# Turning two thirds of an inverse spectrum by copies through DRAM instead of by VectorE, with a new planned order

## The chip, the core and the metric

The kernel runs on one core of a Trainium2 chip. The core has a matrix engine (TensorE, PE in the profile), a vector engine (VectorE, DVE), an activation engine (ScalarE, ACT), a general engine (GpSimd, POOL) and a synchronising engine (SyncE, SP) that here only issues transfers; sixteen DMA engines move data between DRAM and the on-chip memory SBUF. Matmul results land in PSUM. The metric is the time of one execution on the device in microseconds (us), lower being better. The kernel before took 353.0 us in the median of three runs (352.21 to 354.79).

## The reference

Two branches work on the same input `u` (2048 positions, 640 channels) and are mixed by a gate. Branch A is a state-space layer: a kernel `K` of 2048 taps is built for each channel from complex parameters, and `u` is convolved with it by a Fourier transform of length 4096. Branch B is a gated MLP with a spatial matrix `w_sp` of 2048 x 2048.

```python
g = _sigmoid((x * gate_w).sum(-1, keepdims=True))
# A: convolution of u with K by FFT of length 2 L, plus a skip
P = jnp.exp(logdA[:, :, None] * l[None, None, :])
K = jnp.einsum('dn,dnl,dn->dl', Cc, P, dB).real
Yf = rfft2(pad(u)) * rfft2(pad(K))
y = irfft2(Yf)[:, :, 0, :L] + u * Dskip
# B
z = _gelu(jnp.einsum('bsd,df->bsf', x, w_in))
g2 = jnp.einsum('ts,bsf->btf', w_sp, layernorm(z[..., Fh:])) + b_sp
b = jnp.einsum('bsf,fd->bsd', z[..., :Fh] * g2, w_out)
return g * a + (1 - g) * b
```

## The kernel before

**A planner sets the order.** Every piece of work is recorded with `add` (or `dma`, `evac`, `actf`, which call it): the engine or engines that may do it, a cost, what it reads and writes, and a bias. `Plan.run` then goes through a modelled time, picks on each engine the ready task with the highest value of remaining chain plus bias, and emits the instructions in that order. Dependences in the plan are by named keys, such as `("vs", 0, k)`. The emitted program gets its semaphore waits from the tiles' memory, not from these keys. The table `TUNE` at the head of the file adds a number to the bias of single lines (function, line within it, and a loop index or `None`); it was found by a search.

**The convolution.** The 640 channels are split in two groups, `h = 0` with 480 channels and `h = 1` with 160. The transform of length 4096 is done in stages with matmuls:

- `s1_u` (u) and `conv_s1` (K) do the first stage and store its results to the DRAM tensors `FU_d` and `FK_d`. The stage's result is copied out of PSUM by `evac` into `s1u` or `s1k`.
- `conv_s2(h)` runs over 32 values of `k`, singly for `h = 0`, two at a time for `h = 1`. Each step loads its part of the spectra (`fu`, `fk`), does the second stage (`ps_u`, `ps_s2k`, line 1188), multiplies the two spectra on VectorE (`p12`, line 1190), does the first inverse stage with the table `G` (`ps_v`, line 1196), and ScalarE copies it into `X["vs"][h][:, k, :]` (line 1198). So `vs` holds 128 rows by 32 values of `k` by the channels of the group.
- `conv_vt(g)` turns `vs`: within each block of 32 partitions the partition index and `k` change places. VectorE does this in place by 32x32 transposes, two bf16 channels taken as one 32-bit word, 40 channels of one block at a time (line 1204). `g` = 0, 1, 2 are the three lots of 160 channels of `h = 0`, four transposes each; `g` = 3 is `h = 1`.
- `conv_i2(h)` does the last inverse stage with the table `HT` (lines 1278 and 1280), eight groups of output rows for `h = 0` and four for `h = 1`. `i2_out` scales by the gate and adds to branch B's part: VectorE directly from PSUM for one half (line 1212), ScalarE into `tm` and VectorE or GpSimd for the other (lines 1229 and 1231).

**Around it.** Branch B's spatial product (`sp_block`, `ps_g` line 812, `ps_o` line 832) fills PE for most of the time up to 264 us. Its last rows stay in the tile `acc`, the earlier ones go to DRAM (`ob_d`) and are read back before the last stage.

**Transfers.** `dma` issues on SP, or, where `QQ` stands, on SP or POOL as the planner likes. [...]

The order at the end of `main` in which work is recorded:

```python
    conv_s2(0)
    add("NONE", 0.0, open_cv1, w=["cv1"] + par, deps=cva_ids + kf1_ids + t_ids)
    xk, wk = k_expand(1)
    conv_s1(1, xk, wk)
    for g in range(3):
        conv_vt(g)
    conv_s2(1)
    conv_vt(3)
    oo = ob_load()
    conv_i2(0, oo)
    conv_i2(1, oo)
```

Of the kernel before, what the change touches and what calls it, by code (L numbers as in the profile page):

```python
# [25 lines left out]
class Handle:  # L26
# [9 lines left out]


TUNE = {
    ('conv_s1', 15, ('g', 0)): -1398,
    ('conv_s1', 15, None): 3878,  # L40
    ('conv_s2', 35, ('h', 0)): 10715,
    ('conv_s2', 34, ('h', 0)): 12557,
    ('conv_s2', 34, ('h', 1)): 10661,
    ('conv_s2', 28, None): -730,
    ('conv_s2', 42, None): 11507,
    ('eights', 6, None): 22869,
    ('eights', 13, None): 9278,
    ('i2_out', 15, None): 2641,
    ('k_expand', 28, ('h', 1)): -13135,
    ('k_exps', 10, ('c', 4)): -5933,  # L50
    ('k_exps', 10, None): -2461,
    ('k_store', 13, ('h', 1)): -2592,
    ('k_store', 14, None): -14209,
    ('k_store', 6, None): 2313,
    ('k_tables', 31, ('c', 4)): 1745,
    ('k_tables', 31, None): 2593,
    ('k_tables', 32, ('c', 3)): -6618,
    ('k_tables', 32, None): -5389,
    ('k_tables', 41, ('c', 3)): -7569,
    ('k_tables', 29, ('c', 3)): 19395,  # L60
    ('k_tables', 29, ('c', 7)): 107,
    ('k_tables', 29, None): -29059,
    ('k_tables', 6, ('c', 2)): -1107,
    ('k_tables', 6, None): -36,
    ('k_tables', 18, ('c', 5)): 11204,
    ('k_tables', 18, None): 3646,
    ('k_tables', 17, ('c', 3)): -6816,
    ('k_tables', 17, None): 2377,
    ('k_tables', 36, ('c', 0)): 6700,
    ('k_tables', 36, ('c', 7)): -59230,  # L70
    ('k_tables', 36, None): -4043,
    ('k_tables', 38, None): -15448,
    ('main', 151, ('g', 0)): 41152,
    ('main', 151, ('g', 1)): 3118,
    ('main', 151, ('g', 2)): 1052,
    ('main', 149, None): 37766,
    ('main', 148, None): 1429,
    ('main', 147, None): 3632,
    ('main', 156, None): 2671,
    ('main', 159, None): -8713,  # L80
    ('main', 370, None): -17765,
    ('main', 369, None): -1820,
    ('main', 442, None): 125,
    ('main', 445, None): 3317,
    ('main', 413, None): -4292,
    ('quads', 10, None): 798,
    ('s1_u', 13, ('n0', 12)): -14799,
    ('s1_u', 13, ('n0', 2)): -11216,
    ('s1_u', 16, ('n0', 12)): -1100,
    ('s1_u', 16, ('n0', 2)): -2702,  # L90
    ('s1_u', 16, ('n0', 4)): -8304,
    ('s1_u', 16, None): -26814,
    ('s1_u', 20, ('h', 1)): 37644,
    ('s1_u', 3, ('n0', 0)): -28168,
    ('s1_u', 3, None): 2258,
    ('s1_u', 18, ('h', 1)): -33016,
    ('s1_u', 14, None): -24028,
    ('sp_block', 23, ('tb', 4)): -6232,
    ('sp_block', 23, None): 6779,
    ('sp_block', 25, None): 2910,  # L100
    ('sp_block', 20, ('tb', 0)): 13918,
    ('sp_block', 20, None): -32605,
    ('sp_block', 42, ('tb', 4)): -3738,
    ('sp_block', 42, ('tb', 5)): -4450,
    ('sp_block', 47, ('tb', 3)): 6173,
    ('sp_block', 3, ('tb', 1)): -8813,
    ('sp_block', 3, ('tb', 2)): 26644,
    ('sp_block', 3, ('tb', 7)): -26408,
    ('sp_block', 8, None): -13664,
    ('sp_block', 6, None): -1104,  # L110
    ('sp_block', 5, ('tb', 7)): -23479,
    ('sp_block', 5, None): -15147,
    ('tg_build', 15, None): 6085,
    ('tg_build', 20, None): 11595,
    ('x_group', 3, ('g', 0)): -1523,
    ('x_group', 3, ('g', 1)): -4918,
    ('x_group', 3, None): -1876,
    ('z1_tile', 10, ('g', 0)): 17523,
    ('z2_tile', 18, ('h', 1)): -43258,
    ('z2_tile', 10, None): -1119,  # L120
}
HELPERS = ("dma", "actf", "evac", "<lambda>", "ptt", "pts", "ftt", "fts", "pstt", "S_", "E", "K_", "M_")

# [1 line left out]
class Plan:  # L125
# [195 lines left out]
def kernel(  # L321
# [833 lines left out]
    def conv_s2(h):  # L1155
# [6 lines left out]
        for k in range(0, 32, NK):  # L1162
# [86 lines left out]
    def conv_i2(h, oo):  # L1249
        W, dsl = GW[h], slice(GO[h], GO[h] + GW[h])  # L1250
        nn = (1, 2)[h]
        for u, n in enumerate(range(0, NS, 2 * nn)):
# [28 lines left out]
            if u == 0:  # L1281
# [95 lines left out]
```

## Time and profile before

| | busy us | share of the span |
|---|---|---|
| span of the profiled execution | 352.3 | |
| PE matmul | 312.7 | 89% |
| VectorE (DVE) | 285.1 | 81% |
| ScalarE (ACT) | 245.2 | 70% |
| GpSimd (POOL) | 86.3 | 25% |
| transfers: q1 (SP) / q0 (POOL), of 16 DMA engines | 54.89 MB / 4.48 MB | 63.9% / 6.2% |

The busy shares are means over stages that differ much. The page's chain, followed back from the end, spends 49% of the span on PE, 20% on VectorE, 13% on ScalarE and 6% on SP's issues; its largest VectorE lines are the products `p` (line 1190) and the transposes `vs` (line 1204), 5% each. [...]

### The profile page before, as it was taken

The page shows a single profiled execution, that of the slowest core. Times are in us where ns is not written, and L with a number is a line of the kernel's source. Part 1 is how long each engine was busy: PE and PEld are TensorE (multiplying, and loading weights), DVE is VectorE, ACT ScalarE, POOL GpSimd, SP SyncE. Part 2 cuts the span into 40 slices and gives each one's busy share as a digit, 9 for nine tenths or more (in the row PEclk, how much of TensorE's full clock was granted, in tenths as well). Part 3 has the DMA queues.
Part 4 walks back from the last instruction along what each step waited for, and adds up shares of the span by engine and source line. Part 5 has one row for each costly group of instructions (what it writes and reads, how often), then busy time and mean ns, then how long its engine had stood idle before and what let it go on. Part 6 is the DMA issues. An engine that isn't in the chain of part 4 may idle for free.

```text
span 352.3 us, 8350 instructions
## 1 busy us (share of the span) xinstructions
PE 312.7 (89%) x3231; PEld 218.7 (62%) x3237; DVE 285.1 (81%) x560; ACT 245.2 (70%) x440; POOL 86.3 (25%) x107
## 2 busy tenths in 40 slices
PE   3899899989999999999999999699999999709982
PEld 3455455767766877878866988476774334406751
DVE  4079996799899599993799699327669999996985
ACT  1877648999996489999986671327558879604842
POOL 3007242000000041000440063427459200303220
PEclk9999999999999999999899999699999999976998
DMA  7979878788575596686296249989869866372404
GB/s 197 209 135 233 173 195 210 206 144 212 168 186 143 112 181 190 162 198 207 78 117 173 82 61 135 163 231 251 241 186 288 245 199 177 97 220 95 141 28 130
DMA packets 108580, 59.89 MB, mean 170 GB/s; under 512 B 75914, under 2 KB 105002, under 8 KB 108542
## 3 DMA queue, kind: packets, MB, share of 16 engines
q1 hardware_dynamic: 106030, 54.89, 63.9%
q0 software_dynamic: 2512, 4.48, 6.2%
q8 instruction: 25, 0.41, 0.5%
q14 instruction: 13, 0.11, 0.1%
HBM read 25.25 MB, written 19.47 MB: 127 GB/s over the span
## 4 chain that ended last, share of the span: by engine, by line
PE 49%; DVE 20%; ACT 13%; SPq 6%; issue 4%; DMA 4%; ACTq 0%; DVEq 0%
PE ps_g L812 21%; PE ps_o L832 6%; SPq L408 6%; PE ps_z L624 6%; ACT mr L415 5%; DVE p L1190 5%; DVE vs L1204 5%; PE ps_k L1046 3%; PE ps_k L1045 3%; PE ps_s2k L1188 3%; PE ps_v L1196 2%; DVE bst L604 2%; PE ps_s1k L1134 2%; ACT ET L415 1%; ACT L415 1%
## 5 line engine op out<-in xcount | busy, mean ns | idle before, releaser
L812 PE MATMUL ps_g<-wT,z2n 128*128 128x256 bf16 (+1 forms) x896 | 109.2, 278 | 1.7 <-DVE vT L816 1.2
L812 PEld LDWEIGHTS <-z2n 128*128 128x128 bf16 (+1 forms) x896 | 90.8, 104 | 18.7 <-issue 3.9
L1190 DVE TENSOR_TENSOR p<-ps_s2k,us 128x960 bf16<-128x960 f32 (+1 forms) x48 | 48.3, 1042 | 2.0 <-PE ps_s2k L1188 1.0
L993 POOL COPY ET<-mr 128x80 bf16<-128x80 bf16 x7 | 9.8, 1407 | 133.0 <-PE ps_k L1046 126.9
L832 PE MATMUL ps_o<-Wout,vT 128*128 128x320 bf16 (+1 forms) x224 | 33.8, 299 | 0.9 <-DVE vT L818 0.5
L624 PE MATMUL ps_z<-xg,Win 128*128 128x512 bf16 (+1 forms) x134 | 31.2, 379 | 1.4 <-ACT gl L598 1.1
L415 ACT ACTIVATE ET<-ci 128x640 bf16<-128x640 int16 (+1 forms) x40 | 25.7, 678 | 9.5 <-DVE ci L361 9.5
L592 PE MATMUL ps_z<-Win,xT 128*128 128x432 bf16 (+1 forms) x160 | 31.1, 353 | 1.0 <-ACT gl L598 1.0
L1046 PE MATMUL ps_k<-ET 128*32 128x33 bf16 x640 | 28.4, 258 | 3.9 <-issue 3.8
L1046 PEld LDWEIGHTS <-ET 128*32 128x32 bf16 x640 | 27.7, 195 | 3.3 <-issue 3.2
L1045 PEld LDWEIGHTS <-ET 128*32 128x32 bf16 x640 | 27.3, 192 | 2.6 <-issue 1.9
L1045 PE MATMUL ps_k<-ET 128*32 128x33 bf16 x640 | 28.8, 259 | 0.0
L832 PEld LDWEIGHTS <-vT 128*128 128x128 bf16 (+1 forms) x224 | 21.7, 97 | 10.2 <-issue 1.0
L1198 ACT CAST vs<-ps_v 128x480 bf16<-128x480 f32 (+1 forms) x48 | 24.4, 524 | 5.0 <-PE ps_v L1196 4.1
L1196 PE MATMUL ps_v<-p,G 128*128 128x480 bf16 (+1 forms) x128 | 25.2, 303 | 1.6 <-DVE p L1190 0.8
L816 DVE TENSOR_TENSOR vT<-ps_g,br 128x512 bf16<-128x512 f32 (+1 forms) x32 | 19.1, 617 | 8.6 <-PE ps_g L812 8.6
L1188 PE MATMUL ps_s2k<-fk,T 128*128 128x480 bf16 (+1 forms) x128 | 25.1, 306 | 0.2
L592 PEld LDWEIGHTS <-xT 128*128 128x128 bf16 x160 | 15.8, 99 | 15.3 <-issue 2.3
L415 ACT ACTIVATE mr<-lre 128x320 bf16<-128x320 f32 x66 | 25.0, 458 | 0.3 <-DVE ET L1017 0.2
L422 ACT CAST us<-ps_u 128x480 bf16<-128x480 f32 (+1 forms) x48 | 24.1, 523 | 0.8 <-ACT vs L1198 0.6
L624 PEld LDWEIGHTS <-Win 128*128 128x128 bf16 (+1 forms) x140 | 14.2, 101 | 16.1 <-issue 1.4
L422 ACT CAST s1k<-ps_s1k 128x960 bf16<-128x960 f32 (+1 forms) x15 | 13.0, 890 | 16.0 <-PE ps_s1k L1134 5.7
(192 smaller groups left out, 585.1 us busy)
## 6 DMA issues: line engine op xcount, KB each, us to landing
FU_d<-s1u SPq DMA_DIRECT2D x16, 240.0 KB, 3.0
fu<-FU_d SPq DMA_DIRECT2D x16, 240.0 KB, 2.9
fk<-FK_d SPq DMA_DIRECT2D x16, 240.0 KB, 3.0
z_d<-zt SPq DMA_DIRECT2D x24, 128.0 KB, 2.0
z1t<-z_d SPq DMA_DIRECT2D x8, 384.0 KB, 4.6
xf<-in_A_u_dram SPq DMA_DIRECT2D x8, 320.0 KB, 3.4
FK_d<-s1k SPq DMA_DIRECT2D x5, 480.0 KB, 5.4
Win<-in_B_w_in_dram SPq DMA_DIRECT2D x2, 1080.0 KB, 6.0
```

What stands on the lines that cost most here:

```text
L415: return add("ACT", cost, lambda e: act.activation(out=out_(), in_=in_(), func=func, scale=scale), r=r, w=w, fset=fs, bias=bias, deps=deps ...
L422: (vec.tensor_copy if e == "DVE" else act.copy)(out=out_(), in_=in_())
L592: pe.matmul(ps()[:, h, 0:432 + h], lhsT=xT[:, i, 128 * st:128 * st + 128], rhs=Win2[:, i, 432 * h:432 * h + 432 + h], start=(i == 0), stop ...
L624: pe.matmul(ps()[0:fs, ft - f0, :], lhsT=Win1[:, i, 128 * ft:128 * ft + fs], rhs=xg()[:, i, :], start=(i == 0), stop=(i == ND - 1))
L812: pe.matmul(ps()[0:fs, ft - f0, :], lhsT=z2n[:, st, 128 * ft:128 * ft + fs], rhs=wT()[:, st, :], start=(st == 0), stop=(st == NS - 1))
L832: pe.matmul(ps()[:], lhsT=vT[ft // 2]()[0:fs, ft % 2, 128 * r:128 * r + 128], rhs=Wout[0:fs, ft, HD * h:HD * h + HD], start=(ft == 0), sto ...
L1045: pe.matmul(o_, lhsT=ET[:, 0:32, d], rhs=M2[:, :, d], start=True, stop=False, tile_position=(0, 32 * q))
L1046: pe.matmul(o_, lhsT=ET[:, NA:NA + 32, d], rhs=E2[:, :, d], start=False, stop=True, tile_position=(0, 32 * q))
L1188: pe.matmul(ps()[:, i, W * n:W * n + W], lhsT=TK(k + n, i), rhs=fk()[:, j + n, :], start=True, stop=True)
L1190: add("DVE", dv1(2 * NW), lambda e, p12=p12, ps=ps, us=us: vec.tensor_tensor(out=p12()[:, :, 0:NW], in0=ps()[:, :, 0:NW], in1=us()[:, 0:NW ...
L1196: pe.matmul(pv()[:, W * n:W * n + W], lhsT=GV(k + n, i), rhs=p12()[:, i, W * n:W * n + W], start=(i == 0), stop=(i == 1))
L1198: add("ACT", 0.15 + NW / 1170, lambda e, k=k, pv=pv: act.copy(out=X["vs"][h][:, k:k + NK, :], in_=pv()[:, 0:NW].rearrange("p (k d) -> p k ...
```

## The change

Of the 480 channels of `h = 0`, the first 320 (`VD`) are no longer turned by VectorE. Each time four values of `k` have been copied into `vs`, a transfer stores these channels to a new DRAM tensor `VK_d`, whose first index is `k`, whose second is the partition and whose third is the channel. When all eight stores are done, sixteen transfers load them back into the same places of `vs`, now with `k` on the partition and the old partition (within its block of 32) as the second index: for each of four blocks `q`, for each half `w`, and for two groups `m` of eight rows. The last inverse stage of the first eight rows needs the loads of `m = 0` only. The remaining 160 channels are still turned by four VectorE transposes. The purpose is to take eight of twelve transposes off VectorE. At the same time the whole `TUNE` table is replaced by another one, found by a search; every line of it differs.

```diff
 TUNE = {
-    ('conv_s1', 15, ('g', 0)): -1398,
-    ('conv_s1', 15, None): 3878,
-    ('conv_s2', 35, ('h', 0)): 10715,
...
+    ('conv_i2', 37, ('h', 0)): 1844,
+    ('conv_i2', 39, ('h', 1)): -2564,
+    ('conv_i2', 39, None): -6223,
...
 }
...
     FK_d = [dram.tile([16, 4, 2, 32, w], BF, name=f"FK_d{w}") for w in GW]
+    VD = 320
+    VK_d = dram.tile([32, P, VD], BF, name="VK_d")
...
             add("ACT", 0.15 + NW / 1170, lambda e, k=k, pv=pv: act.copy(out=X["vs"][h][:, k:k + NK, :], in_=pv()[:, 0:NW].rearrange("p (k d) -> p k d", k=NK)), r=[pv, "cvb"], w=[("vs", h, k)], bias=S2E)
+            if h == 0 and k % 4 == 3:
+                dma(QQ, lambda k=k: VK_d[k - 3:k + 1, :, :].rearrange("k m d -> m k d"), lambda k=k: X["vs"][0][:, k - 3:k + 1, 0:VD], 1024 * VD, r=[("vs", 0, k - z) for z in range(4)], w=[("VK", k // 4)], bias=S2B, run=2 * VD)
+
+    def conv_vd():
+        NG = 2
+        g4 = 16 // NG
+        for m in range(NG):
+            for q in range(4):
+                for w in range(2):
+                    i0 = 16 * w + g4 * m
+                    dma(QQ, lambda q=q, i0=i0: X["vs"][0][32 * q:32 * q + 32, i0:i0 + g4, 0:VD], lambda q=q, i0=i0: VK_d[:, 32 * q + i0:32 * q + i0 + g4, :], 1024 * VD // NG,
+                        r=[("VK", i) for i in range(8)], w=[("vd", q, m, w)], bias=6500, run=640)
...
-            vk = [("va", 3, b) for b in range(4)] if h else [("va", g, b) for g in range(3) for b in range(4)]
+            vk = [("va", 3, b) for b in range(4)] if h else [("va", g, b) for g in range(VD // 160, 3) for b in range(4)] + [("vd", q, n // 8, w) for q in range(4) for w in range(2)]
...
-    for g in range(3):
+    conv_vd()
+    for g in range(VD // 160, 3):
         conv_vt(g)
```

More of the change, by code (lines that the diff above doesn't have):

```diff
@@ L38 @@
 TUNE = {
-    ('conv_s1', 15, ('g', 0)): -1398,
-    ('conv_s1', 15, None): 3878,
-    ('conv_s2', 35, ('h', 0)): 10715,
[L42 to L120, printed above, removed]
+    ('conv_i2', 37, ('h', 0)): 1844,
+    ('conv_i2', 39, ('h', 1)): -2564,
+    ('conv_i2', 39, None): -6223,
@@ new lines @@
+    ('conv_s2', 43, None): -17523,
+    ('conv_s2', 35, ('h', 0)): 633,
+    ('conv_s2', 35, ('h', 1)): 993,
+    ('conv_s2', 34, ('h', 0)): 24993,
+    ('conv_s2', 34, None): -4152,
+    ('conv_s2', 27, ('h', 0)): 2880,
+    ('conv_s2', 14, None): -40,
+    ('conv_s2', 28, None): -7269,
+    ('conv_s2', 42, None): -2974,
+    ('conv_vt', 4, None): -1249,
+    ('eights', 6, None): -4248,
+    ('i2_out', 7, None): -4434,
+    ('k_exps', 7, None): 83,
+    ('k_exps', 10, ('c', 0)): -406,
+    ('k_exps', 10, ('c', 4)): 573,
@@ new lines @@
+    ('k_store', 14, None): -2870,
+    ('k_store', 6, ('h', 1)): -12388,
+    ('k_store', 6, None): 8586,
+    ('k_sub', 23, None): -10732,
+    ('k_sub', 13, None): -11315,
+    ('k_tables', 31, ('c', 3)): 220,
+    ('k_tables', 31, ('c', 5)): 1445,
+    ('k_tables', 31, ('c', 7)): -6456,
+    ('k_tables', 41, None): -2285,
+    ('k_tables', 30, ('c', 3)): -7154,
+    ('k_tables', 29, ('c', 1)): 6497,
+    ('k_tables', 29, ('c', 2)): -3535,
+    ('k_tables', 29, ('c', 4)): -18229,
+    ('k_tables', 29, None): -762,
@@ new lines @@
+    ('k_tables', 18, None): -19435,
+    ('k_tables', 17, ('c', 2)): -12249,
+    ('k_tables', 17, ('c', 4)): -5119,
+    ('k_tables', 36, None): -11081,
+    ('k_tables', 20, ('c', 0)): -19918,
+    ('k_tables', 20, None): 6756,
+    ('k_tables', 21, None): -17729,
+    ('main', 153, ('g', 0)): 386,
+    ('main', 153, None): 1913,
+    ('main', 157, None): 1007,
+    ('main', 151, None): 3607,
+    ('main', 359, None): 1898,
+    ('main', 371, None): -18999,
+    ('main', 434, None): -211,
+    ('main', 417, None): 337,
@@ new lines @@
+    ('main', 421, None): -10346,
+    ('main', 426, None): -4607,
+    ('quads', 6, None): -3335,
+    ('s1_u', 13, ('n0', 0)): 3712,
+    ('s1_u', 13, ('n0', 2)): -778,
+    ('s1_u', 13, ('n0', 8)): 1854,
+    ('s1_u', 13, None): -10863,
+    ('s1_u', 16, ('h', 1)): -4227,
+    ('s1_u', 20, ('h', 1)): -1896,
+    ('s1_u', 3, ('n0', 0)): -2236,
+    ('s1_u', 3, None): 1530,
+    ('s1_u', 18, None): -4151,
+    ('s1_u', 14, None): -38867,
+    ('sp_block', 23, ('tb', 2)): 2780,
+    ('sp_block', 25, ('tb', 4)): -4691,
@@ new lines @@
+    ('sp_block', 25, ('tb', 6)): -3589,
+    ('sp_block', 25, ('tb', 7)): -3310,
+    ('sp_block', 25, None): -634,
+    ('sp_block', 20, ('tb', 5)): 5109,
+    ('sp_block', 20, None): -7447,
+    ('sp_block', 42, None): -17740,
+    ('sp_block', 47, None): -17689,
+    ('sp_block', 3, ('tb', 0)): 6151,
+    ('sp_block', 3, ('tb', 1)): 5386,
+    ('sp_block', 3, None): -4487,
+    ('sp_block', 8, None): -8681,
+    ('sp_block', 6, ('tb', 3)): -4753,
+    ('sp_block', 6, None): 7590,
+    ('sp_block', 5, None): 5037,
@@ L121 @@
+    ('tg_build', 9, ('c', 1)): -7818,
+    ('x_group', 3, None): 1651,
+    ('z1_tile', 10, None): 1132,
+    ('z1_tile', 15, ('g', 1)): 2402,
+    ('z2_tile', 18, ('h', 1)): -17771,
 }
```

## The prediction

> **What bounds the kernel now.** I read the busy table by stages first, to see which stage leaves an engine unused, then the chain of waits in the worst stage, then the waits and groups there. Columns of the stage table: stretch, its length, busy time of PE, PEld, DVE, ACT and POOL, granted clock, DMA share, GB/s.
>
> ```profile
> core 0: us, PE busy (x) PEld busy (x) DVE busy (x) ACT busy (x) POOL busy (x), PEclk, DMA share, GB/s
> 60.00:120.00 60.00, 56.31 (x564) 43.45 (x564) 52.27 (x111) 52.44 (x86) 0.51 (x1) 1.00 0.71 170
> ...
> 264.00:304.00 40.00, 38.04 (x181) 16.54 (x180) 39.13 (x39) 34.20 (x68) 11.19 (x17) 1.00 0.73 210
> 304.00:318.00 14.00, 2.94 (x19) 1.80 (x18) 13.39 (x12) 1.90 (x3) 2.71 (x3) 0.79 0.67 187
> 318.00:338.00 20.00, 19.45 (x180) 14.12 (x179) 16.74 (x22) 13.71 (x33) 5.46 (x5) 0.89 0.31 96
> 338.00:352.30 14.30, 6.33 (x46) 4.29 (x44) 9.56 (x19) 4.71 (x12) 2.94 (x3) 0.91 0.33 97
> ```
>
> Up to 264 us PE is nearly always busy, so a new order there can win or lose only a few us. From 264 to 304 (spectrum product of the first 480 channels) PE and DVE are both full. From 304 to 318 only DVE works: this is the stage that the change attacks. The chain of waits (start, us, what) names it:
>
> ```profile
> 302.78 0.82 DVE s1k L422
> 303.61 0.07 DVE vs L1204
> 303.67 1.01 issue
> 304.69 12.71 DVE vs L1204 x11
> 317.40 0.04 issue
> 317.44 1.76 PE ps_i L1280 x4
> ```
>
> Twelve VectorE transposes stand between the last eviction into vs480 (ends 303.1) and the first inverse matmul (317.4). The waits after 304 show who stands still, the groups what one piece costs:
>
> ```profile
> PE ps_i L1280 <- DVE vs L1204: 10.5, 1, 10.5
> ...
> L1190 DVE TENSOR_TENSOR p<-ps_s2k,us 128x960 bf16<-128x960 f32 x32 | 35.4, 1152 | 0.7 <-ACT us L422 0.2 <-PE ps_s2k L1188 0.2
> L1204 DVE STREAM_TRANSPOSE vs<-vs 128x640 f32<-128x640 f32 x16 | 18.6, 1326 | 0.0
> ...
> L1190 DVE TENSOR_TENSOR p<-ps_s2k,us 128x640 bf16<-128x640 f32 x16 | 12.9, 822 | 1.3 <-PE ps_s2k L1188 0.8
> ```
>
> The DMA issue list gives prices for a trip through DRAM:
>
> ```profile
> FK_d<-s1k POOLq DMA_DIRECT2D x3, 480.0 KB, 7.1
> ...
> fu<-FU_d SPq DMA_DIRECT2D x8, 160.0 KB, 2.2
> ```
>
> **What the skill says.** "VectorE: DVE Perf Modes", The three transpose paths: the VectorE transpose turns 32x32 blocks only, and a plain strided DMA is a bad transpose when the innermost stride is large. The trace has the former at 1.33 us per 128x640; the new copies keep contiguous runs of 640 bytes, so the warning does not bite. "DMA: Bandwidth & Descriptors", Anatomy of one DMA: about 2.0 us fixed, most of it the receipt of the last byte, plus bytes / 436e3. That estimates 2.8 us for 320 KB, but POOL's 480 KB stores took 7.1 us (the formula says 3.1), so I take traced landings. "Trainium Kernel Development and Optimization", Key Constraints: transfers of all queues run on the same 16 DMA engines; the trace agrees in that the best 4 us stretches end at 288 to 328 GB/s with a share of 1.00 to 1.10. "Trainium Architecture — The Big Picture", Inside one NeuronCore: each engine has its own instruction stream and meets others only at semaphores. So what stands behind a waiting VectorE instruction waits too.
>
> **The change, part by part.** *Removed:* 8 of the 12 transposes. Back to back they took 12.71/11 = 1.16 us, so VectorE loses 8 x 1.16 = 9.2 us, all on the path.
>
> *Added:* 8 stores of 320 KB from vs480, one per four k, all on POOL, and 16 loads of 160 KB back, 9 on SP and 7 on POOL: 2.62 MB each way. POOL computes nothing on the path there; its issues cost 0.53 us (loads) to 0.91 us (stores) in the groups. Seven of the eight stores lie beside the spectrum product. The stage of 264 to 304 already moves 8.4 MB at a share of 0.73.
>
> *Moved:* the order of the built program differs everywhere. Three things count. (a) 21 output matmuls (ps_o) come after instead of before the first product matmul: 21 x 0.137 us (0.95 per 7 in the chain) = 2.9 us less ahead, so the first product comes at 264.2 - 2.9 = 261.3, if the stages before are neutral. (b) The second convolution's first stage moves into the product stage. Between the first product and the last of the 32 of the first 480 channels VectorE now has 32 products, 6 s1k copies (0.82), 3 acc copies (0.55), one vT product (0.3) and 2 sign flips, instead of 32 products, 2 copies and 2 flips: 5.2 us more on 37.65 (264.2 to 301.85), 42.9 us. Eviction follows 1.2 us later: last vs480 written at T = 261.3 + 42.9 + 1.2 = 305.4, against 303.1. PE gains a similar 5 to 6 us of work. (c) In return 16 product steps of the last 160 channels no longer wait: in before their kernel spectrum was loaded only at 312.5. They can fill the turn.
>
> *The wait that it adds.* The built program has semaphore waits that the data does not need: the four remaining transposes write channels 320 to 479, the copies touch 0 to 319, but they lie in one tile, and the program orders them. VectorE's order after T is product, product, transpose 1, product, transpose 2, two products, transpose 3, two products, transpose 4, six products, inverse evictions. Transpose 1 waits for all 8 stores; the first 9 loads wait for transpose 3; transpose 4 waits for those 9 loads; the other 7 loads wait for transpose 4. The first inverse matmuls wait for the first half of the loads, and the products queued behind transposes 1 and 4, and PE behind them, stand still. By step:
> - Products done at T+1.1. Last store: issue 0.9 and landing 2.5 (fastest FK_d) to 7.2; I take 3.7, so T+4.6. Stall 3.5.
> - Three transposes of 1.3 and three products of 0.8: T+10.9.
> - Nine loads, 1.47 MB: 4.5 us at the best stretch's 328 GB/s, 7 us at the stage's 210; I take 5.6, plus 2.5 us of latency as the shortest fk load: T+19. Two products fill 1.6; stall 6.5.
> - Transpose 4 and six products: T+25.2. The 7 loads behind (4.4 + 2.5) are hidden beside them.
> - Rest of VectorE: 2 products 1.6, 8 evictions of 480 at 0.72, 8 of 160 at 0.3, 3 or more adds 1.4, 4 transposes 4.9: 16.1. Waits among them 3 (before had 3.5 in 12.85 us after its last product), last store to end 3.45 as before: T+47.8.
>
> Before had T+49.2. The 9.2 us that VectorE is relieved of come back as 3.5 + 6.5 us of standing still. T itself is 2.3 us later by work, and I add 2 us for DMA: stores (2.3 MB), the second spectrum's store and load (2.6 MB) on top of 8.4 MB are 13.3 MB in 44 us, 302 GB/s, where the best 4 us stretches had 288 to 328; three buffers of two steps each hide some of it. Nothing added costs 0, saturation up to 6. So 305.4 + 2 + 47.8 = 355.2 us.
>
> The rest of the new order (first loads, tables, blocks up to 261 us) moves work among full engines: 9 us of PE idle from 60 to 240 can be won, or as much lost; no sign in the profile decides, so 0, with plus or minus 4 in the range.
>
> **The rivals.** *Faster, 346 us.* Stores land at 2.5 us, the nine loads need 5.5 in all, so the stalls are 2.3 and 4; no DMA slowdown; the early part gives 2 to 4 us. 305.4 + 44.1 - 3.5 = 346. For it: the 14 us hole with PE, ACT and half of DMA idle is real, and the second convolution now fills it. Against: nine loads with two issuing queues, 164 KB each, in 5.5 us is 268 GB/s with no latency.
> *Slower, 361 us.* The product stage is bound by DMA: +6; the last store lands at 7 us behind queued loads, stall 6; PE cools down in the stalls (its granted clock was 0.50 to 0.52 from 312 to 320 after its idle stretch). 305.4 + 6 + 50 = 361. For it: 302 GB/s asked; 16 small xk loads stand on SP ahead of the fk loads of the later steps. Against: part of these bytes falls after T, where DMA is freer (0.31 from 318 to 338).
> A third, the turn hidden entirely and all VectorE relief kept (343), needs the extra semaphore waits to be void, which the order denies.
>
> **How the numbers follow.** The middle case 0.38, faster 0.30, slower 0.32. Forecast 355 us, within 1% of 353.0 (349.5 to 356.5). The range runs from 344 (faster rival and 2 us of early gain) to 362 (slower rival and a little): about 2 in 10 lies outside. The middle case spreads over the upper bound too, so faster by over 1% 0.30, within 1% 0.35, slower by over 1% 0.35.
>
> **What would show it.** In the profile after: 4 transposes of vs480, the first preceded by a VectorE wait of about 3.5 us on a DMA, the fourth by about 6.5 us on loads; no stretch of 10 us without PE; the product stage longer by 5 to 7 us with a share near 0.95; last vs480 eviction near 307. I am wrong if the transposes start without such waits (then 343 to 346), if fk or fu loads land later than 5 us and hold products (then 360), or if the product stage begins more than 4 us away from 261.

## The result and the profile after

The changed kernel took 371.8 us (median of 4 runs, 367.1 to 374.7) beside 353.5 for the kernel before: a ratio of 1.044 with a 95% interval of 1.032 to 1.055. It is slower by 4%; the forecast was 355.0 with a range of 344 to 362.

The profile taken with this result has TensorE at a lower granted clock (0.938) than the kernel's other executions (0.947 to 0.960), so the lines below are of a further run of the changed kernel (span 370.0 us, clock 0.952). I cut every span in three, at two instants read from the trace's instruction list: the start of the first product `p` of 960 columns, and the end T of the 32nd eviction into vs480 (the part of `vs` with the 480 channels of `h = 0`).

| us | up to the first product | product stage, up to T | from T to the end | span |
|---|---|---|---|---|
| kernel before | 264.2 | 38.9 | 49.2 | 352.3 |
| forecast | 261.3 | 46.1 | 47.8 | 355.2 |
| changed kernel | 269.3 | 49.3 | 51.4 | 370.0 |

The product stage of the kernel before, and the busy table of the changed kernel by stages, columns as in the prediction:

```profile
264.20:303.10 38.90, 37.44 (x178) 16.26 (x177) 38.20 (x38) 33.11 (x67) 11.11 (x17) 1.00 0.73 210
```

```profile
0.00:269.30 269.30, 243.99 (x2796) 179.77 (x2797) 207.59 (x469) 189.78 (x321) 66.39 (x83) 0.97 0.75 169
269.30:318.60 49.30, 41.71 (x219) 20.33 (x219) 42.80 (x47) 34.54 (x69) 16.37 (x23) 1.00 0.91 271
318.60:330.00 11.40, 7.23 (x63) 6.32 (x62) 8.47 (x10) 5.11 (x13) 1.67 (x3) 0.74 0.28 80
330.00:337.00 7.00, 1.55 (x16) 1.35 (x14) 0.12 (x1) 1.20 (x3) 1.42 (x3) 0.74 1.09 221
337.00:345.00 8.00, 4.63 (x36) 4.43 (x36) 4.96 (x6) 2.82 (x7) 1.74 (x3) 0.53 0.61 139
345.00:370.00 25.00, 16.83 (x112) 10.78 (x112) 16.18 (x28) 10.09 (x23) 7.96 (x8) 0.90 0.36 109
```

The stage that was full before (VectorE 38.20 of 38.90) now leaves VectorE idle for 6.5 of 49.3 us. The 14 us in which only VectorE worked are gone; in their place stand 7 us in which hardly anything but the DMA engines works (330 to 337; TensorE 1.55 us), and TensorE is at 0.53 of its clock behind them. The chain of waits names both stops of the turn:

```profile
318.86 3.57 DMA VK_d<-vs
322.81 1.11 issue
...
324.70 1.20 DVE vs L1217
...
329.08 1.36 POOL vs L411 x3
330.83 7.24 DMA vs<-VK_d
338.51 1.00 issue
```

The last store lands before the first of the four transposes may start, and the fourth transpose stands until the first nine loads have landed. The waits from 318 to 345 have their sizes (total, times, longest), and the groups of the product stage by shape show what VectorE does there:

```profile
DVE vs L1217 <- DMA vs<-VK_d: 8.2, 1, 8.2
...
DVE vs L1217 <- DMA VK_d<-vs: 2.8, 1, 2.8
```

```profile
L1191 DVE TENSOR_TENSOR p<-ps_s2k,us 128x960 bf16<-128x960 f32 x32 | 35.2, 1150 | 6.0 <-ACT us L423 3.6 <-PE ps_s2k L1189 2.3
...
L423 DVE CAST s1k<-ps_s1k 128x640 bf16<-128x640 f32 x6 | 4.7, 814 | 0.0
L360 DVE TENSOR_SCALAR acc<-ps_o,omg 128x320 bf16<-128x320 f32 x3 | 1.7, 550 | 0.2
```

A product is as fast as before (1150 against 1152 ns), but 6.0 us pass in front of products where it was 0.7. So about 5 us are lost before the products, 10 in them and 2 behind them. The experiments ask what each of the three is: the new biases or the turn, bytes or order.

### The profile page after: what moved, and what is told of

Same layout as the page of the kernel before. It is cut to its first block, busy times and chain, and to the rows that moved or that the text cites. A ratio compares the mean times of both kernels' runs of the same rounds, so it can differ in the third digit from the quotient of the medians.

```text
span 372.9 us, 8387 instructions
## 1 busy us (share of the span) xinstructions
PE 317.9 (85%) x3237; PEld 223.8 (60%) x3237; DVE 280.1 (75%) x556; ACT 243.3 (65%) x434; POOL 95.5 (26%) x121
## 4 chain that ended last, share of the span: by engine, by line
PE 56%; DMA 17%; DVE 12%; ACT 5%; issue 5%; SPq 2%; POOL 1%; DVEq 0%; ACTq 0%
PE ps_g L813 17%; PE ps_z L593 8%; PE ps_z L625 6%; PE ps_o L833 6%; DVE p L1191 5%; PE ps_k L1046 4%; PE ps_k L1047 3%; PE ps_v L1197 3%; DMA xf<-in_A_u_dram 3%; PE ps_s2k L1189 2%; DMA xT<-in_A_u_dram 2%; PE ps_s1k L1135 2%; DMA Wout<-in_B_w_out_dram 2%; DMA vs<-VK_d 2%; DMA xk<-KA_d 2%
## 5 line engine op out<-in xcount | busy, mean ns | idle before, releaser
L813 PE MATMUL ps_g<-wT,z2n 128*128 128x256 bf16 (+1 forms) x896 | 112.0, 281 | 4.8 <-DVE vT L817 3.5
L813 PEld LDWEIGHTS <-z2n 128*128 128x128 bf16 (+1 forms) x896 | 91.7, 104 | 22.4 <-issue 5.9
L1191 DVE TENSOR_TENSOR p<-ps_s2k,us 128x960 bf16<-128x960 f32 (+1 forms) x48 | 47.6, 1037 | 8.3 <-PE ps_s2k L1189 4.1
L994 POOL COPY ET<-mr 128x80 bf16<-128x80 bf16 x6 | 8.0, 1341 | 130.8 <-PE ps_k L1047 100.0
L1197 PE MATMUL ps_v<-p,G 128*128 128x480 bf16 (+1 forms) x128 | 27.3, 322 | 15.8 <-DVE p L1191 13.7
L833 PE MATMUL ps_o<-Wout,vT 128*128 128x320 bf16 (+1 forms) x224 | 35.2, 307 | 0.0
L833 PEld LDWEIGHTS <-vT 128*128 128x128 bf16 (+1 forms) x224 | 22.5, 100 | 8.9
L1197 PEld LDWEIGHTS <-G 128*128 128x128 bf16 x128 | 11.8, 107 | 25.5 <-DVE p L1191 17.3
L625 PEld LDWEIGHTS <-Win 128*128 128x128 bf16 (+1 forms) x140 | 14.0, 101 | 15.4 <-issue 0.6
```

Source lines behind the costliest of these rows:

```text
L625: pe.matmul(ps()[0:fs, ft - f0, :], lhsT=Win1[:, i, 128 * ft:128 * ft + fs], rhs=xg()[:, i, :], start=(i == 0), stop=(i == ND - 1))
L813: pe.matmul(ps()[0:fs, ft - f0, :], lhsT=z2n[:, st, 128 * ft:128 * ft + fs], rhs=wT()[:, st, :], start=(st == 0), stop=(st == NS - 1))
L833: pe.matmul(ps()[:], lhsT=vT[ft // 2]()[0:fs, ft % 2, 128 * r:128 * r + 128], rhs=Wout[0:fs, ft, HD * h:HD * h + HD], start=(ft == 0), sto ...
L1191: add("DVE", dv1(2 * NW), lambda e, p12=p12, ps=ps, us=us: vec.tensor_tensor(out=p12()[:, :, 0:NW], in0=ps()[:, :, 0:NW], in1=us()[:, 0:NW ...
```

## The experiments

All times beside the kernel before on the same chip; parts as in the table above.

| run | median us | ratio to before [95%] | first product | stage | rest |
|---|---|---|---|---|---|
| e0_after | 369.3 | 1.043 [1.032, 1.054] | 269.3 | 49.3 | 51.4 |
| e1_old_order_turn | 371.3 | 1.047 [1.041, 1.054] | 263.1 | 49.0 | 56.8 |
| e2_new_order_no_turn | 369.6 | 1.043 [1.036, 1.051] | 269.3 | 47.6 | 52.7 |
| e3_loads_first | 363.4 | 1.024 [1.018, 1.031] | 275.9 | 49.3 | 44.7 |
| e4_old_order_loads_first | 359.2 | 1.013 [1.010, 1.017] | 262.6 | 49.0 | 42.8 |
| e8_old_order_quarter_turn | 366.7 | 1.035 [1.026, 1.043] | 263.4 | 49.0 | 50.8 |
| e7_new_order_xk_pool | 371.5 | 1.036 [1.026, 1.046] | 265.9 | 47.1 | 51.7 |
| e6_old_vd480 | 355.4 | 0.997 [0.994, 1.000] | 263.6 | 49.5 | 38.3 |
| e10h_order_kept | 366.4 | 1.034 [1.028, 1.039] | 263.0 | 38.9 | 62.6 |
| e10i_order_kept_loads_first | 372.3 | 1.052 [1.046, 1.058] | 269.9 | 38.9 | 64.8 |
| e10f_vd480_order_kept | 369.0 | 1.043 [1.037, 1.048] | 265.1 | 40.2 | 60.8 |
| e13_new_early_old_late | 367.1 | 1.027 [1.020, 1.034] | 263.4 | 43.8 | 54.0 |
| e15_order_kept_loads_pool | 374.5 | 1.055 [1.049, 1.060] | 264.5 | 40.4 | 68.3 |
| f3i_s1k_spread | 367.9 | 1.039 [1.033, 1.044] | 261.3 | 43.1 | 59.7 |
| f4i_s1k_spread_early | 369.0 | 1.041 [1.036, 1.046] | 264.0 | 43.8 | 58.6 |
| g1_spread_loads_pool | 361.1 | 1.015 [1.005, 1.026] | 265.7 | 43.3 | 50.4 |
| g2_spread_vd320 | 361.1 | 1.018 [1.009, 1.027] | 268.5 | 43.1 | 50.8 |

A profile is one execution. The profiled one of e3 was 8 us longer than its median, and reached the first product 6.6 us later than e0 in the same order, so only its last two parts are used. The profiled ones of e7 and e13 were 5 and 4 us shorter than their medians.

### The two halves of the change alone

e0 repeats the changed kernel. e1 keeps its code and takes the old biases, e2 keeps the code of before and takes the new biases:

```diff
 TUNE = {
-    ('conv_i2', 37, ('h', 0)): 1844,
...
+    ('conv_s1', 15, ('g', 0)): -1398,
...
```

> The changed kernel itself again, for a profile at the undisturbed clock and as the partner of the other runs: about 369 us, first p12 product at about 269 us, last vs480 eviction at about 318 us, 50 us from there to the end. Both theories expect the same of it.

> The turn through DRAM alone, under the biases of the kernel before. Theory A (the loss is the new order: some 10 us before the first product and some 8 us in the product stage; the turn gives about what it costs): 350 to 357 us, first p12 within 3 us of the kernel before's 264.2, product stage within 3 us of its 38.9, and 47 to 52 us from the last vs480 eviction to the end. Rival B (the loss is the traffic of the turn, 5.2 MB more, which slows the loads that feed TensorE and queues behind them): 362 us or more, with the product stage longer than 45 us.

> The new biases alone: all 480 channels turned by VectorE as in the kernel before, no store and no load of the turn. Theory A (the order): 364 to 371 us, first p12 at 269 us or later, product stage 46 us or more. Rival B (the traffic of the turn): 350 to 356 us, product stage back to about 39 to 44 us, since nothing of the turn moves.

Each theory got one run right (e1 came out as rival B said, e2 as theory A), so neither is the whole cause: each half alone costs what both cost together, 4.7%, 4.3% and 4.3%. The turn alone makes the product stage 10 us longer, and the new biases without a byte of turn make it 9 us longer; together they make it 10 us longer, not 19. With the new biases the turn changes the total by less than the measurement tells (369.3 against 369.6). That the three totals agree is in part chance: e1 loses another 7.6 us behind T, e2 5.1 ahead of the first product and 3.5 behind T.

### The turn's waits behind the last eviction

e3 and e4 plan the four VectorE transposes behind all 16 loads, e3 in the changed kernel, e4 with the old biases:

```diff
-                r=[("vs", h, k) for k in range(0, 32, (1, 2)[h])], w=[("va", g, b)], bias=8000)
+                r=[("vs", h, k) for k in range(0, 32, (1, 2)[h])] + ([("vd", q, m, w) for q in range(4) for m in range(2) for w in range(2)] if h == 0 else []), w=[("va", g, b)], bias=8000)
```

> The changed kernel with the four VectorE transposes of channels 320 to 479 planned behind all 16 loads of the turn, so that no load waits for a transpose of other channels of the tile; everything up to the last vs480 eviction is the same. Theory A (order upstream, and behind the last eviction two waits by tile, 3.5 + 6.5 us): 4 to 9 us less than the changed kernel, 41 to 46 us from the last vs480 eviction to the end in place of 50. Rival C (the loads themselves are the price, 16 loads at some 0.5 us of issue and 2.6 to 7.1 us of landing): within 2 us of the changed kernel, since the inverse products then wait for the transposes behind the loads.

> The old biases with the turn, and the four VectorE transposes planned behind all 16 loads. The earlier runs split the span in three: to the first product, the product stage up to the last vs480 eviction, and the rest: 264.2 + 38.9 + 49.2 in the kernel before, 263.1 + 49.0 + 56.8 in the old order with the turn. If the three parts are independent, this one is 263 + 49 + 45 (the 45 from the run with the loads first) = 357 us, still slower than before, by the product stage alone. If the loads cost something by themselves wherever the transposes stand, the last part stays over 50 and the time over 363.

Both came out as the first theory said: the rest falls by 6.7 us (51.4 to 44.7) and by 14.0 (56.8 to 42.8). The stage table of e4 behind T:

```profile
311.60:327.00 15.40, 12.73 (x153) 10.32 (x151) 11.56 (x15) 11.48 (x30) 4.83 (x8) 1.00 0.86 184
```

TensorE works in 12.7 of these 15.4 us, and its clock stays at 1.00 in them. The 16 products of the last 160 channels run at once (310.3 to 326.2 in e4; 310.8 to 350.2 in e1, behind transposes that wait for transfers). So this order of transposes and loads, which wait for each other through the one tile and not through the data, costs 7 to 14 us with the products that stand behind it. Even so e4 stays 1.3% slower than before: in its profile the other two parts are shorter than before, and the product stage is 10.1 us longer.

### Bytes or order in the product stage

e8 moves a quarter of the turn's bytes with every instruction in its place; three quarters of the turned values are left out:

```diff
-... VK_d[k - 3:k + 1, :, :].rearrange("k m d -> m k d"), lambda k=k: X["vs"][0][:, k - 3:k + 1, 0:VD], ...
+... VK_d[k // 4:k // 4 + 1, :, :].rearrange("k m d -> m k d"), lambda k=k: X["vs"][0][:, k:k + 1, 0:VD], ...
```

> The old order with the turn, every store and load at its place and with its waits, but each store moves one of its four rows and each load 8 of its 32 partitions (80 KB in place of 320 KB a store): three quarters of the turned channels' values are left out. Theory D (the product stage is longer because the stores' bytes fill the DMA engines, 0.90 busy against 0.74, and fu and fk land later): the stage falls from 49.0 to 44 us or less, the time by 5 us or more. Rival E (not the bytes, but the places in the queues, or the work of the last 160 channels that now lies in the stage: two stores FK_d, four loads fk1, more casts): the stage stays at 47 us or more.

The rival won: 49.0 us again. The intervals between successive products are the same one by one (the long ones 2.66, 1.91, 3.64, 2.30, 3.66 in e1, and 2.68, 1.91, 3.64, 2.30, 3.65 in e8). A stage that keeps its pattern to 0.02 us when only a quarter of the turn's bytes moves is not waiting for these bytes.

e10h then keeps the bytes and restores the order. The planner charges a transfer to a single pipe (in short `s = max(end + 1.0, dma); dma = s + nb`), so a priced store can push the modelled fk and fu loads back, and the planner then fills TensorE with something else. With the store's price taken out and its bias at the bottom (both at once; which of the two does it was not separated), TensorE's instructions in this stage stand exactly as in the kernel before:

```diff
-... 1024 * VD, r=[("vs", 0, k - z) for z in range(4)], w=[("VK", k // 4)], bias=S2B, run=2 * VD)
+... 1, r=[("vs", 0, k - z) for z in range(4)], w=[("VK", k // 4)], bias=-30000, run=2 * VD)
```

> The old biases with the turn of 320 channels, its stores priced in the planner at one byte and given the lowest bias, so that TensorE's order in the product stage is the kernel before's, instruction for instruction, while the chip moves the full 320 KB a store. Theory G (the stage grew from 38.9 to 49.0 us because the planner, which charges a store 's time to one DMA pipe, put the products into another order: ps_v of two steps, then ps_s2k of two, with all eight ps_s1k groups between them; the bytes do nothing): the stage is 39 to 42 us, and with the waits of the turn left in the rest, 263 + 41 + 52 = 356. Rival D (the traffic): the stage stays over 46 us and the time over 364.

The stage is 38.9 us, as in the kernel before, with the full 320 KB in every store. The time, 366.4, missed the 356 that was expected: the rest took 62.6 us in place of 52 (next section). The three stage lines side by side, of e1, e8 and e10h:

```profile
263.10:312.10 49.00, 40.16 (x197) 17.72 (x196) 40.64 (x41) 35.05 (x70) 17.31 (x24) 1.00 0.90 267
```

```profile
263.40:312.40 49.00, 40.15 (x198) 17.73 (x197) 40.64 (x41) 35.01 (x70) 16.01 (x24) 1.00 0.80 233
```

```profile
263.00:301.90 38.90, 37.43 (x178) 16.29 (x177) 38.21 (x38) 33.12 (x67) 14.94 (x22) 1.00 0.90 271
```

Read the DMA share before the last number: 0.90, 0.80, 0.90. The two long stages differ in traffic, and the short one has the traffic of the first. Not all of the 10.1 us is waiting, for e1 has eight `ps_s1k` groups (the first stage of `K` for the last 160 channels) ahead of T, and e10h and the kernel before have five: VectorE works 2.4 us more in e1 (40.64 against 38.21) and is idle for 8.4 us against 0.7. What the order does is seen in the timeline of e8 (start, length, engine, instruction; in brackets the idle time ahead and who ended it):

```profile
304.41 0.58 PE L1198 MATMUL ps_v<-p,G 128*128 128x480 bf16 x2 [0.19 <-DVE p L1192]
304.83 0.97 PE L1190 MATMUL ps_s2k<-fk,T 128*128 128x480 bf16 x4
305.50 2.22 DVE L1192 TENSOR_TENSOR p<-ps_s2k,us 128x960 bf16<-128x960 f32 x2 [1.15 <-PE ps_s2k L1190]
306.72 0.56 PE L1190 MATMUL ps_s2k<-fk,T 128*128 128x480 bf16 x2 [0.91 <-DVE p L1192]
```

TensorE's order has `ps_v` of a step, which needs the product, ahead of the `ps_s2k` of the next steps, which feed it. So TensorE waits for VectorE, then issues two steps of `ps_s2k`, and VectorE has waited 1.15 us. The kernel before, and e10h, roll (`ps_s2k`, `ps_v`, `ps_u`, one step each), and VectorE waits 0.7 us in all.

### Where the kept order gives it back

e10i is e10h with the transposes behind the loads, e10f turns all 480 channels (`VD = 480`, no transpose of vs480 left), e6 is the same under the priced stores.

> The old order with all 480 channels turned through DRAM, so that no transpose of vs480 is left on VectorE: stores of 480 KB, loads of 480 KB. If the stores' bytes set the product stage, it grows from 49.0 by about another 4 to 6 us, to 53 or more; after the last eviction no load waits for a transpose and no transpose for a load, so the rest falls from 56.8 to 42 to 47. Sum 263 + 54 + 45 = 362. If bytes do not matter, the stage stays at 49 and the sum is 357 or less.

> The same with the four transposes behind the 16 loads. Theory G: stage 39 to 42; the rest was 42.8 with the work of the last 160 channels begun before the last eviction; here that begins after it, as in the kernel before, so I expect 43 to 47: 263 + 41 + 45 = 349, faster than before by about 1%. Rival D: 357 or more.

> All 480 channels turned through DRAM, no transpose of vs480, stores unpriced, so the product stage in the kernel before's order. Theory G: stage 39 to 43 (480 KB a store), the rest 40 to 44: 263 + 41 + 42 = 346, about 2% faster than before. Rival D (bytes): the stage is the longest of all, over 49, and the time over 353.

e6 equals the kernel before (0.997, interval 0.994 to 1.000): stage 49.5, rest 38.3, so its stage did not grow with 1.5 times the bytes and the sum was better than I expected. e10i and e10f confirm the stage (38.9, and 40.2 with stores of 480 KB) and miss in the rest: over 60 us where I expected 40 to 47. The products of the last 160 channels begin 28 to 30 us behind T in e10h and e10f, against 17 before and at once in e6. Their kernel spectrum comes by the chain `ps_s1k`, store FK_d, load fk1 (the four loads of that spectrum). Under the kept order six of the eight `ps_s1k` groups lie around T (300 to 304 us in e10h, 301 to 305 in the kernel before), and the chain then meets the turn's loads. The DMA lists of e10h (302 to 332) and of the kernel before (303 to 322), with issue to landing last:

```profile
vs<-VK_d SPq DMA_DIRECT2D x9, 160.0 KB, 7.6
fk<-FK_d SPq DMA_DIRECT2D x4, 320.0 KB, 11.1
```

```profile
fk<-FK_d SPq DMA_DIRECT2D x4, 320.0 KB, 3.2
```

The four loads are issued at 319 to 322 in place of 312.5 to 314, behind the turn's on the same queue, and take 11.1 us in place of 3.2. (The inverse matmuls, which stand ahead of these products in TensorE's order, wait too: 15.6 us for the turn's loads.) e15 gives all 16 loads of e10f to GpSimd's queue:

```diff
-                E_[e].dma_start(out=out_(), in_=in_())
+                E_[on or e].dma_start(out=out_(), in_=in_())
...
+    on="POOL")
```

> The run with all 480 channels turned and the product order kept (40.2 us of product stage, then 60.8), with one edit: the nine loads of the turn that stood on SyncE's queue ahead of the four fk1 loads are issued by GpSimd. Theory H (the gain of the kept order was given back because the four fk1 loads, issued at 312.5 in the kernel before, stood behind the turn's loads and started at 319; the products of the last 160 channels then began 28 us after the last eviction in place of 17): the first product of the last 160 channels comes 16 to 20 us after the last vs480 eviction, the rest falls from 60.8 to 48 to 53, the time to 352 to 358. Rival (the DMA engines are full, whoever issues): still 25 us or more, the time within 2% of 369.

Theory H failed as put: the rest grew to 68.3. Both marks of the rival were met: the first product of the last 160 channels comes 35.1 us behind T, and 374.5 us is within 2% of 369. fk1 did start at 315.8, but its last load took 21.5 us and landed at 338.7, and the DMA share was 1.02 to 1.03 from 310 to 339 with one queue issuing the turn. TensorE's order also has inverse matmuls ahead of these products, and they waited for loads of the turn that were issued until 326.7 and landed until 338.3. The place in the queue was at most one obstacle of several.

### Eight groups in a rolling order, and the DMA bill

f3i and f4i take e10f, release one `ps_s1k` group every second product from step 12 (every third from step 6), and plan the inverse products behind the products of the last 160 channels:

```diff
-... w=[ps], bias=7500, hold_=[so])
+... w=[ps], bias=7500 + (12000 if h else 0), hold_=[so], deps=[mvs[12 + 2 * (4 * g + 2 * ab + j)]] if h else ())
...
-... m, r=["HT"] + vk, w=list(dict.fromkeys(pr)), bias=6000)
+... m, r=["HT"] + vk, w=list(dict.fromkeys(pr)), bias=6000, deps=() if h else [mvs[46]])
```

> All 480 channels turned; stores unpriced so that ps_s2k, ps_v and ps_u keep the kernel before's rolling order up to step 12, and from there one ps_s1k group every second product (eight in the stage instead of the kernel before's three and five behind); inverse products planned behind the products of the last 160 channels. Theory I (what the stage loses is the order in pairs, not the eight ps_s1k groups themselves, 0.8 us of VectorE or 0.7 of ScalarE each): stage 42 to 44, the next products start at once, the rest 38 to 41 as in the earlier run with 480 channels: 263 + 43 + 39 = 345, 2% faster than before. Rival J (the eight groups in one ring of two PSUM buffers with ps_s2k are the price): stage 48 or more, 350 or more in all.

> The same with one ps_s1k group every third product from step 6 on. Theory I: 42 to 44 us of product stage and 345 us; if xk is not loaded that early, TensorE waits in order for it and the stage is longer by those waits. Rival J: 48 or more.

Theory I holds for the stage: 43.1 and 43.8 us with all eight groups in it (the kernel before has five of them ahead of T, not three as expected here), 6 us less than in pairs. g2, below, has 43.1 too with e1's stores of 320 KB. So of the 10 us that the turn adds to the stage in e1, some 4 go with the groups that moved into it and some 6 with the order. The rest missed by 20 us, and the profile of f3i says why. Its stage line from 315 to 332, and its DMA list from 311 to 331:

```profile
315.00:332.00 17.00, 0.73 (x8) 0.60 (x9) 0.00 (x0) 0.55 (x2) 0.48 (x1) 0.60 1.02 222
```

```profile
vs<-VK_d SPq DMA_DIRECT2D x9, 240.0 KB, 7.2
vs<-VK_d POOLq DMA_DIRECT2D x7, 240.0 KB, 11.7
fu<-FU_d SPq DMA_DIRECT2D x3, 160.0 KB, 14.2
```

For 17 us hardly any engine works and the DMA engines are full: they move 3.8 MB at 222 GB/s, most of it the turn's, and the fu loads issued behind land only at the end. g1 issues the turn's loads on GpSimd alone, as in e15; g2 does that with 320 channels, its four transposes planned behind the products.

> The run with the eight ps_s1k groups spread over the rolling order (43.1 us of product stage, then 59.7) showed all engines idle from 315.8 to 332.6 while the DMA engines were full with the turn's loads (4.1 MB at 205 GB/s) and three fu loads behind them took 14.2 us to land. Here all 16 loads of the turn are issued by GpSimd, so that the fu loads on SyncE's queue do not stand behind them. If the queue was the cause, the products of the last 160 channels run from 307 to about 328 and the time is 347 to 352; if the full DMA engines are, fu still lands after 8 us or more and the time is 356 or more.

> The same with 320 channels turned through DRAM as in the change, 2.6 MB of stores and 2.6 MB of loads in place of 3.9 and 3.9, and the four VectorE transposes of the other 160 planned behind the products of the last 160 channels. If full DMA engines are the cause, the stretch of idle engines behind the last eviction is a third shorter than in the run with 480 channels, and the four transposes give 4.6 us of that back. If the queue is, it equals the other run within 3 us, plus the 4.6 us of transposes.

g1 gains 9.3 us of rest (59.7 to 50.4): the queue. The remainder is not the queue: from 319.5 to 333.5 its DMA share is 1.03, and TensorE works 6.34 of 14 us. The first two fu loads behind T land in 2.8 and 2.2 us, but the next two, issued beside the turn's 16 loads, take 7.9 and 11.4 us, and TensorE waits for both:

```profile
326.06 0.31 PE L1183 MATMUL ps_u<-fu,T 128*128 128x160 bf16 x2 [2.42 <-DMA fu<-FU_d]
332.35 0.45 PE L1183 MATMUL ps_u<-fu,T 128*128 128x160 bf16 x2 [4.09 <-DMA fu<-FU_d]
```

So the marks for full DMA engines (8 us or more, 356 or more) were reached, by the last of the loads and by the time, 361. g2, with a third fewer bytes, agrees: its fu loads take up to 7.2 us, TensorE waits 2.4 us for them in place of 6.8, and the last product ends 22.4 us behind T in place of 27.1. The four transposes that it has to do besides give this back (rest 50.8 against 50.4). No version beats the kernel before; e6 equals it.

### The new order by itself

e7 is e2 with the 16 xk loads of the last 160 channels issued by GpSimd, by the same edit as in e15, and all compute orders the same. e13 takes, without the turn, the old biases for the convolution's products, transposes and inverse products and for its first stage of `K`, and the new ones for the rest; every engine's order is that of e2 up to about 233 us.

> The new biases without the turn, the order on TensorE, VectorE and ScalarE the same, but the 16 small loads xk of the last 160 channels that stood in one block on SyncE's queue (274.9 to 283.2 us in the run without the turn, 0.42 us of issue each plus their waits) are issued by GpSimd. Theory F (that block holds up three fk and three fu loads behind it, whose buffers were free some 6 us earlier): the product stage falls from 47.6 to 41 to 44 us and the time by 3 to 7 us. Rival (the loads wait for their buffers, not for the queue; or ps_s1k on TensorE now waits for xk): within 2 us.

> No turn; the new biases for everything up to the convolution's products, the old ones for the products, the transposes and the inverse products. Theory A (the new order loses before the first product, by waits of TensorE that add to 7 us, and again in the product stage, by its own order there): first product at 266 to 270, the stage back near 41 to 43 (21 ps_o matmuls more than in the kernel before lie in it), the rest 49: 357 to 361. If the early loss comes from the late biases or is noise, the first product is at 264 and the time 353 to 355.

e7 refutes theory F: loads that stood behind the block left up to 6 us earlier, counted from the first product, and the stage stayed at 47.1. TensorE's order, the same in e2 and e7, is what is left to hold the time there; no run shows it directly. e13 fits neither of its cases: the first product came at 263.4, the stage at 43.8, and the rest was 54.0 in place of 49. In e0, e2, e7 and e13 one interval between two products, from the 12th to the 13th, is 6.46, 6.40, 5.91 and 6.14 us, against 1.16 before. The timeline of e0 shows what stands in it:

```profile
283.23 1.12 PE L833 MATMUL ps_o<-Wout,vT 128*128 128x320 bf16 x7
...
284.83 2.28 DVE L423 CAST s1k<-ps_s1k 128x640 bf16<-128x640 f32 x3
...
287.47 1.12 PE L833 MATMUL ps_o<-Wout,vT 128*128 128x320 bf16 x7
...
288.42 0.97 PE L1189 MATMUL ps_s2k<-fk,T 128*128 128x480 bf16 x4
```

The output matmuls that the new order moved behind the first product, with `ps_s1k` groups between them, form one block of 5 us in TensorE's order, and no `ps_s2k` is issued in it. The interval in e0 as a stage line:

```profile
283.77:290.23 6.46, 6.23 (x40) 3.67 (x38) 5.26 (x9) 3.15 (x7) 2.52 (x3) 1.00 0.99 341
```

TensorE and VectorE are busy in most of it, so the block is moved work more than waiting. The same holds of the stage: of the new order's 8.7 us (47.6 less 38.9, e2), 4.1 are work of VectorE that was moved in (42.34 against 38.20) and 4.6 are idle time (5.2 against 0.7). e13 keeps the block under the old late biases and has 3.1 us more work and 1.7 more idle time than the kernel before.

Before the first product the spread between executions is large. TensorE's order there is one and the same in all thirteen profiles of the old order, that of the kernel before among them (its trace lacks six records): 261.3 to 265.7 us in eleven of them, 269.9 and 268.5 in e10i and g2, 264.5 in the mean. In the new order it is one and the same in e0, e2 and e7: 269.3, 269.3 and 265.9. TensorE's mean clock up to there was 0.97 in e0, e2, e10i and g2, and 0.98 or 0.99 in the others, so single times can't be compared. TensorE's idle time ahead of the first product (stretch less busy time) separates the two orders: 25.3 (e0), 25.0 (e2) and 25.4 us (e7), against 17.2 to 22.5 with the old order (18.1 in the kernel before, 19.8 in the mean). So the new order costs some 2.5 to 8 us of standing still, 5.4 between the means. Against this stand 21 output matmuls fewer ahead of the first product, 2.9 us by the prediction's price. Two of the waits that grew, in e0:

```profile
PE ps_s1x L656 <- DMA xf<-in_A_u_dram: 4.6, 2, 2.5
PE ps_g L813 <- DVE vT L817: 3.8, 3, 2.2
```

The second is 3.8 us in all three and 1.1 to 2.1 with the old order. The first overlaps (2.5 and 3.5 in e2 and e7, 1.8 to 4.3 with the old order). e13, whose order is the new one up to about 233 us, came to the first product with 22.0 us of idle time, inside the old order's range. So which part of the early order does it, and how much the clock adds, stays open.

## Why the prediction was wrong

The forecast ran 14.8 us short of the profile: 8.0 before the first product, 3.2 in the stage, 3.6 behind T.

- **"If the stages before are neutral", first product at 261.3.** This step failed by most: 269.3. The moved matmuls are there, but TensorE stands still for 25.3 us ahead of the first product, against 18.1 before and 17.2 to 22.5 in all profiles of the old order, and its clock is a little lower (0.97 against 0.98). I put this term at nothing, with 4 us either way, because nothing decided the sign; the changed kernel (269.3) and e7 (265.9) were both beyond that.
- **Product stage, VectorE's work.** From the first product to the end of the last, 42.9 us were forecast, 0.5 of them waits taken over from before. VectorE worked 41.8 us there, so the list of what moved into the stage was right; but the stretch took 48.1.
- **Product stage, "I add 2 us for DMA".** This term was wrong in size and in cause. VectorE's idle time in the stage is 6.5 us, and e2 has 5.2 (47.59 less 42.34) without any turn. e8 and e10h show, under the old biases, that 320 KB a store cost the stage nothing, at a share of 0.90. I had seen that "the order of the built program differs everywhere" and counted what moved, not the sequence in which TensorE would come to it.
- **The waits behind T.** The mechanism was right: 2.8 us on the last store (3.5 forecast), 8.2 us on the loads (6.5), the fourth transpose at T+19.7 (T+19). e3 and e4 confirm that this order costs 7 and 14 us. (The 2.5 us quoted as the fastest landing of a store was that of a load; the fastest store had taken 3.6 in the profile before, and the last one here took 3.6. So the faster rival's stall of 2.3 us had no trace behind it.)
- **"Rest of VectorE", T+47.8.** From the fourth transpose on it took 31.7 us, not 28.8. VectorE worked 21.1 us of it (22.2 forecast) and 4.1 passed behind its end (3.45), so the term that was too small is the 3 us of waits: 6.5. The Trainium skill, "TensorE: Matmul & The Clock Gate", Part 1, has the clock fall to half after an idle window of about 3.4 us. The trace agrees here: behind the idle stretch 330 to 337 the granted clock is 0.53 from 337 to 345, and it is 1.00 from 311.6 to 327 in e4, where TensorE's longest stop is 1.2 us. It is not the whole rule, for earlier in e0 the clock fell to 0.50 (98.7 to 102.1) behind a stop of 2.2 us. That the lower clock made these waits longer was not tested by itself; I had named it in the slower rival only.
- **The rivals.** The slower one (361) had the right sign. Of its reasons the cooled TensorE was seen, and DMA saturation of the stage was not what made the stage longer. That the turn be worth nothing net was right under the new biases (e0 against e2), but the biases were not neutral; without them the turn alone cost 4.7%.

## What to carry to other kernels

Where a planner sets the order, one added transfer can change the order of engines that it does not touch. Before blaming the transfer, hold the order of the compute engines fixed and change the bytes, then hold the bytes and restore the order. When steps are pipelined over a small ring (a few buffers used in turn), look in the in-order engine's sequence for a consumer that stands ahead of the next producers; the sum of busy times does not show it. A gain on one side of a stage boundary (38.9 against 49.0 us here) is worth nothing until the next stage's inputs, their place in the queues and the DMA time that they share are followed as well.

## What was not expected of the hardware

- 2.3 MB of stores beside the products, at a DMA share of 0.90, cost the stage nothing (38.9 us with and without them in e10h and the kernel before), though single stores took 3.2 to 5.2 us to land. With 3.4 MB (e10f, e15) it was 40.2 and 40.4 us, at 0.93 and 0.94.
- The way back is dearer than the way out. At a full share the loads of the turn came to 217 to 222 GB/s (g1, f3i), while the product stage of f3i moved 301 GB/s at 0.96. GpSimd's queue in g1 shows it alone, first in the product stage (43.3 us, nearly all stores of the turn), then while the turn's loads ran (316.7 to 338.8); the columns are packets, MB and share of the 16 engines:

```profile
q0 software_dynamic: 1440, 3.77, 26.2%
```

```profile
q0 software_dynamic: 768, 3.93, 83.1%
```

That is 3.0 us of all engines for a MB out and 4.7 us for a MB back. Why is not shown; each load writes 32 partitions, each store reads 128. A 240 KB load took 7.2 to 11.7 us in the medians of f3i's two queues, 16 of them issued within 4.2 us; the formula that the prediction quotes from the Trainium skill ("DMA: Bandwidth & Descriptors", Anatomy of one DMA) estimates 2.6 us for one.
- One instruction stream, up to the first product, took between 261.3 (f3i) and 269.9 us (e10i) in profiles of the old order, with a mean clock of 0.99 and 0.97: TensorE was busy for 243.1 and 249.0 us and idle for 18.2 and 20.9.
